# The state's decay diagonal in eight pieces, mean squares by halves, and nine fewer products of constants at the start of a fused RWKV-5 and SwiGLU kernel

## The chip, the cores and the metric

The kernel runs on one core of a Trainium2 chip. The metric is the time of one execution on the device in microseconds (us). Every time of a kernel below is a median over several executions on one chip; times within a kernel are read from one profiled execution. Every run told here was in the fast state. The profile is of one execution, and its span is about 1.8 us shorter than that execution's time (653.1 against 654.93 for one of the changed kernel).

## The reference, cut to what matters

A linear-attention recurrence over 768 steps (4 batches, 8 heads of 48) gives 3072 tokens of 384 features, which go through RMS normalisation and a gated feed-forward layer with 1536 hidden features, all in float32.

```python
for t in range(S):
    kt, vt, rt = (k[:, :, t], v[:, :, t], r[:, :, t])
    cur = np.einsum('bhd,bhe->bhde', u[None] * kt, vt)
    y[:, :, t] = np.einsum('bhd,bhde->bhe', rt, state + cur)
    state = w[None, :, :, None] * state + np.einsum('bhd,bhe->bhde', kt, vt)
# ... y becomes x, (3072, 384)
rms = np.sqrt(np.mean(x * x, axis=-1, keepdims=True) + 1e-06)
xn = x / rms * rms_g
g = xn @ w_gate
silu = g * (1.0 / (1.0 + np.exp(-g)))
return silu * (xn @ w_val) @ w_out
```

## The kernel before

The tokens are cut into 12 blocks of 64 steps (256 tokens with the four batches). The first blocks run while the weights of the feed-forward layer still arrive: they come as 64-bit numbers and are rounded by ScalarE, VectorE and GpSimd together. For this part, which lasts some 155 us, the kernel does not fix the order of the instructions by hand. It describes each piece of work with its engine, an estimated duration, what it reads and what it writes, and a small search at build time looks for a good order:

```python
class Plan:
    HOP = 0.2
    def add(self, engine, cost, reads, writes, give, land=0.0, port=False, name=""):
        ...
    def run(self, cells, first, free, idle=None, trials=3000):
        ...
        rng, best = random.Random(3), None
        for trial in range(trials):
            new = dict(goals)
            ...                                    # a random change of the goals
            start = self.schedule(new, free)
            end = self.replay(start, free)
            end = max(end[i] for i in cells) + 0.3 * sum(end[i] for i in cells) / len(cells)
            if best is None or end <= best[0]:
                best, goals = (end, start), new
        self.start = best[1]
        busy = free["PE"]
        for i in sorted(range(len(self.ops)), key=lambda i: (self.start[i], i)):
            if self.ops[i][0] == "PE":
                if idle and busy < first:
                    idle(self.start[i] - busy)     # products of constants into the gap
                busy = self.start[i] + self.ops[i][1]
            self.ops[i][3]()
```

So every change of a duration or of a dependence can change the order on all engines. The search's `cells` are the two kinds of large products: a gate product (two of them, for the gate and the value, each of 12 passes that use half of the array's rows, 64 of 128) and an output product (12 passes on all 128 rows).

```python
def product(ps_, w, x, start):                     # a gate product: 12 passes of 64 rows
    for cc in range(CC):
        for z in range(2):
            rows = slice(64 * z, 64 * z + 64)
            pe.matmul(ps_[:, z, 0:NT], w[rows, cc, :], x[rows, cc, :], ...)

def add_cell(s, i, hs):                            # an output product: 12 passes of 128 rows
    ...
    for j in range(2):
        for o in range(NQ):
            pe.matmul(po[:, j, 0:DM], hs[o][0][:, j * P : (j + 1) * P], wo[i][:, o, :], ...)

def gate_val(s, i, o):
    # ... two products, then
    add("ACT", 0.38, keys, [f"h{n}"], ..., name=f"silu {s}")
    add("DVE", 0.42, keys, [f"h{n}"], ..., name=f"hm {s}")    # gate times value
```

The parts that the change touches are the diagonal of the state's decay, the mean squares, and the products of constants that keep TensorE warm in the gaps of the first 25 us:

```python
def state_decay():
    for z in range(2):
        rows = slice(64 * z, 64 * z + D)
        for p in range(HP):
            act.mul(KH[rows, z, :, p, :], ...)     # eight instructions of ScalarE

def mean_squares(bank, sq):
    for half in range(2):
        for i in range(CC):
            pe.matmul(bank[:, 2 * P + half : 2 * P + half + 1],
                      sq[:, i, half * P : (half + 1) * P], ones[:, 0:1], ...)

add("ACT", 3.0, ["pw"], ["khd"], state_decay, name="khd")
...
add("PE", 1.35, ["sq0", "sq1"], [key], lambda bank=bank: mean_squares(bank, sq), name=f"r {s}")
...
def warm(us):
    for _ in range(int((us - 0.3) / 0.22)):
        pe.matmul(gv["c"][:, 0, 0:P], ones, ones, start=True, stop=True)
```

Of the kernel before, what the change touches and what calls it, by code (L numbers as in the profile page):

```python
# [49 lines left out]
P = 128  # L50
# [4 lines left out]
def free_dims(t, *dims):  # L55

    return bass.AP(tensor=t.tensor, offset=t.offset, ap=[list(t.ap[0])] + [list(d) for d in dims])
# [3 lines left out]
B, H, S, D = 4, 8, 768, 48  # L61
HP = H // 2
L = 64
NS = S // L
DM, DFF = H * D, 1536
CC = DM // P
# [27 lines left out]
class Plan:  # L94
# [8 lines left out]
    def add(self, engine, cost, reads, writes, give, land=0.0, port=False, name=""):  # L103

        deps = {self.last[r] for r in reads if r in self.last} | {self.last[w] for w in writes if w in self.last}
        for w in writes:
            deps |= self.readers.get(w, set())
        n = len(self.ops)
        if engine in ("DVE", "ACT"):
            cost += 0.03  # L110
        self.ops.append((engine, cost, deps, give, land, port, name))
        for w in writes:
            self.last[w], self.readers[w] = n, set()
        for r in reads:
            if r not in writes:
                self.readers.setdefault(r, set()).add(n)
        return n
# [89 lines left out]
def fast(ctx, tc, chan, tok, vpad, wka, wkb, wot, cols, u_row, out, bad):  # L207
# [8 lines left out]
    pe, dve, act, pool, sp = (InOrder(tc, e) for e in (nc.tensor, nc.vector, nc.scalar, nc.gpsimd, nc.sync))  # L216
# [28 lines left out]
    ones = c_tile([P, P], "ones")  # L245
    dve.memset(ones, 1.0)
    pw = raws.tile([P, HP, L], FP32, name="pw")
# [6 lines left out]
    KH = c_tile([P, 2, B, HP, D], "KH")  # L254
    TOK = c_tile([P, 2, B, HP, D], "TOK")

    ident = c_tile([P, P], "ident")
# [4 lines left out]
    for z in range(2):  # L262
        rows = slice(64 * z, 64 * z + 64)
# [19 lines left out]
    pows = {1: wcol}  # L283
# [20 lines left out]
        act.copy(wk[64:128], ps[64:128, :, 0:D])  # L304
        act.copy(wk[0:64], ps[0:64, :, 64 : 64 + D])

    def state_decay():

        for z in range(2):
            rows = slice(64 * z, 64 * z + D)  # L310
            for p in range(HP):
                act.mul(
                    KH[rows, z, :, p, :], free_dims(ident[rows, 64 * z : 64 * z + D], (0, B), (1, D)),
                    pows[L][rows, p : p + 1],
                )

    def w_range():

# [205 lines left out]
        act.copy(xb[s][64 - 64 * z : 128 - 64 * z], xa[s][64 * z : 64 * z + 64])  # L524


    def mean_squares(bank, sq):
        for half in range(2):
            for i in range(CC):
                pe.matmul(  # L530
                    bank[:, 2 * P + half : 2 * P + half + 1], sq[:, i, half * P : (half + 1) * P], ones[:, 0:1],
                    start=i == 0, stop=i == CC - 1, skip_group_check=True,
                )

    def root(bank, ms):
        act.activation(ms, bank[:, 2 * P : 2 * P + 2], AF.Sqrt, scale=1.0 / DM, bias=eps)
# [65 lines left out]
    p = Plan()  # L602
    add = p.add
# [11 lines left out]
        i = turn["at"] % 2  # L615
        return at[i], f"at{i}"

    add("SP", 0.3, [], ["w"], lambda: None, land=1.9)
    add("DVE", 2.4, ["w"], ["pw"], powers, name="powers")
    add("DVE", 0.43, ["pw"], ["up"], lambda: dve.tensor_mul(up, pw, by_inv), port=True)  # L620
    add("DVE", 0.43, ["pw"], ["down"], lambda: dve.tensor_mul(down, pw_rev, by_inv), port=True)
    add("DVE", 0.22, [], ["dmask"], lambda: dve.tensor_add(dmask, ident[:, 0:64], ident[:, 64:128]), port=True)
# [5 lines left out]
    bank, key = next_at()  # L628
    add("PE", 0.9, ["gdup"], [key], lambda bank=bank: token_powers(bank), name="wk")
    add("ACT", 0.7, [key], ["wk"], lambda bank=bank: keep_token_powers(bank), name="wk")  # L630
    add("ACT", 3.0, ["pw"], ["khd"], state_decay, name="khd")

    def loads(s):
        if s == 0:
# [14 lines left out]
    def mixing(s):  # L649
# [76 lines left out]
                name=f"yT {s}",  # L726
            )
        bank, key = next_at()
        add("PE", 1.35, ["sq0", "sq1"], [key], lambda bank=bank: mean_squares(bank, sq), name=f"r {s}")
        add("ACT", 0.3 if s == 0 else 2.9, [key], ["ms"], lambda bank=bank: root(bank, ms), name=f"sqrt {s}")  # L730
        add("DVE", 0.45, [], ["ms", "diag"], lambda: inverse(ms, diag), name=f"inv {s}")
        add("PE", 0.45, ["diag"], [key], lambda bank=bank: spread(bank, diag), name=f"spread {s}")
# [10 lines left out]
        for z in range(2):  # L743
            add("DVE", 0.95, ["TOKk", "wk"], [f"KH{z}"], lambda z=z: state_k(s, z), port=True, name=f"h {s}")
        last = [next_at() for _ in range(2)]
        add(
            "PE", 1.9, ["KH0", "KH1", "khd", "VSv", "VSs0", "VSs1"], [last[0][1], last[1][1]],
            lambda: [states(last[half][0], half) for half in range(2)], name=f"U {s}",
        )
        for half in range(2):  # L750
# [100 lines left out]

    def warm(us):

        for _ in range(int((us - 0.3) / 0.22)):
            pe.matmul(gv["c"][:, 0, 0:P], ones, ones, start=True, stop=True)

    p.run(cells, 25.0, {"PE": 1.5, "DVE": 1.5, "ACT": 2.5, "POOL": 6.3, "SP": 1.8}, warm)
# [698 lines left out]
```

## Time and profile before

| | before |
|---|---|
| time, median of three | 654.4 us (654.15 to 655.77) |
| span of the profiled execution | 653.1 us |
| TensorE busy | 98% of the span |
| first real product | 9.49 us |
| second load of chan (keys and receptances, by feature) issued, landed | 14.81, 20.46 us |
| first weights product | 27.38 us |
| first output product | 46.4 us |
| main part (the same order in both kernels) begins | 155.8 us |

All but the median are read from the profile. The prediction shows the lines and says how to read them. In the lines, first_a to first_c and at are buffers of sums, hbuf holds gate times value, xa the normalised tokens, wa, wb and wo the weights, and raw, bits and ulp are weights on their way from 64-bit numbers. Three things matter: TensorE has no gap between 52 and 182 us, so the start can only shift what follows; the start is ruled by a chain over DMA, VectorE and ScalarE and not by TensorE; and the DMA engines are nearly full in the first 20 us (a share of 0.90 up to 20.46). One reading was missed then and is shown here, the timeline of TensorE around the first output product. Its columns are start, length, engine, line, work, passes, and in brackets the idle time before it and what ended that:

```profile
44.91 1.50 PE L91 MATMUL at<-ones,sq_first 128*128 128x1 f32 x12 [1.66 <-ACT sq_first L91]
46.27 5.81 PE L91 MATMUL first_b<-wo,hbuf 128*128 128x384 f32 x12
51.92 0.59 PE L91 MATMUL at<-diag,ones 128*128 128x256 f32 x2
```

The output product (second line) takes 5.7 us at half clock instead of about 4. What follows it (third line) needs the diagonal of the inverse root mean squares, which VectorE began at 49.78 and had done at 49.78 + 1.73 = 51.51. With the usual 0.14 us to start, the third line could not have begun before 51.65. So the half clock costs this order only about 0.3 us (an estimate from these lines).

### The profile page before, as it was taken

The numbers are of one execution on the slowest core, as the hardware profiler recorded it, in microseconds if no ns is written. First come the engines' busy times: TensorE is split into PE (matmuls) and PEld (weight loads), VectorE is DVE, ScalarE is ACT, GpSimd is POOL, SyncE is SP. The second block draws the span as 40 slices with busy tenths as digits, with TensorE's granted clock in tenths as the row PEclk, the third lists the DMA queues.
The fourth block names the chain that finished last, engine by engine and source line by source line (L and its number), as shares of the span: only waits on it lengthen the run. The fifth ranks groups of instructions, "written<-read, shape, count | busy, mean of one in ns | idle before, by whom it ended". The sixth has DMA issues, their size and how long they took to land.

```text
span 653.1 us, 15289 instructions
## 1 busy us (share of the span) xinstructions
PE 638.6 (98%) x6534; PEld 504.7 (77%) x6534; DVE 384.7 (59%) x560; ACT 341.9 (52%) x952; POOL 41.7 (6%) x39
## 2 busy tenths in 40 slices
PE   9889999999999999999999999999999999999996
PEld 8868777787878766889766888866888966788753
DVE  6988878855765734765743576653576562555400
ACT  5695465944364653574672564673555582433400
POOL 3154423100000000000000000000000000000000
PEclk9999999999999999999999999999999999999999
DMA  8786643053004242204331404332312321122211
GB/s 260 254 310 213 194 116 115 12 170 78 27 3 167 61 138 49 75 22 166 98 111 40 110 20 158 93 93 73 93 37 101 106 73 25 42 63 73 55 27 28
DMA packets 20398, 64.50 MB, mean 99 GB/s; under 512 B 2912, under 2 KB 6112, under 8 KB 18912
## 3 DMA queue, kind: packets, MB, share of 16 engines
q1 hardware_dynamic: 20320, 63.42, 32.3%
q8 instruction: 53, 0.87, 0.6%
q14 instruction: 25, 0.20, 0.1%
HBM read 58.69 MB, written 4.72 MB: 97 GB/s over the span
## 4 chain that ended last, share of the span: by engine, by line
PE 86%; DVE 5%; ACT 4%; issue 2%; DMA 1%; POOL 0%; DVEq 0%; ACTq 0%; POOLq 0%; SPq 0%
PE po L91 24%; PE b L91 15%; PE a L91 10%; PE c L91 9%; PE first_c L91 5%; PE first_b L91 5%; PE first_a L91 5%; PE at L91 4%; PE py L91 4%; PE pa L91 2%; PE pu L91 2%; ACT ME L91 1%; DVE TOK L91 1%; ACT MO L91 1%; DVE gv L91 1%
## 5 line engine op out<-in xcount | busy, mean ns | idle before, releaser
L91 PE MATMUL po<-wo,h 128*128 128x384 f32 x480 | 159.8, 489 | 0.8 <-DVE bad L91 0.8
L91 PEld LDWEIGHTS po<-wo,h 128*128 128x128 f32 x480 | 90.0, 190 | 60.2 <-PE pc L91 0.8
L91 DVE TENSOR_TENSOR gv<-b,m 128x512 f32<-128x512 f32 x90 | 62.1, 690 | 84.2 <-PE b L91 83.5
L91 ACT ACTIVATE gv<-gv 128x512 f32<-128x512 f32 (+1 forms) x60 | 31.0, 518 | 52.9 <-DVE gv L91 52.9
L91 DVE TENSOR_TENSOR gv<-c,gv 128x512 f32<-128x512 f32 x60 | 41.4, 690 | 15.0 <-PE c L91 14.0
L91 ACT COPY o<-po 128x384 f32<-128x384 f32 x20 | 9.5, 474 | 77.4 <-PE po L91 39.2
L91 ACT ACTIVATE ME<-dmask,du 64x64 f32<-64x64 f32 x176 | 43.8, 330 | 9.8 <-DVE du L91 9.4
L91 PE MATMUL a<-xa,wa 64*128 64x256 f32 x360 | 45.0, 383 | 0.7 <-DVE h L91 0.7
L91 PE MATMUL b<-xa,wa 64*128 64x256 f32 x360 | 44.4, 379 | 0.6 <-DVE gv L91 0.6
L91 ACT ACTIVATE MO<-dmask,du 64x64 f32<-64x64 f32 x176 | 44.4, 334 | 0.7 <-DVE du L91 0.3
L91 PE MATMUL c<-xb,s 64*128 64x256 f32 x360 | 44.3, 378 | 0.0
L91 PE MATMUL b<-t,wb 64*128 64x256 f32 x360 | 44.3, 378 | 0.0
L91 PE MATMUL b<-t,s 64*128 64x256 f32 x360 | 44.0, 377 | 0.3 <-DVE gv L91 0.3
L91 PE MATMUL a<-xb,wb 64*128 64x256 f32 x360 | 43.9, 376 | 0.0
L91 PE MATMUL c<-t,s 64*128 64x256 f32 x360 | 43.9, 376 | 0.0
L91 PEld LDWEIGHTS a<-xa,wa 64*128 64x128 f32 x360 | 33.8, 187 | 7.2 <-DVE h L91 3.0
L91 PEld LDWEIGHTS b<-xa,wa 64*128 64x128 f32 x360 | 34.2, 187 | 6.1 <-DVE gv L91 2.4
L91 PEld LDWEIGHTS b<-t,s 64*128 64x128 f32 x360 | 34.8, 187 | 4.7 <-DVE gv L91 0.7
L91 PEld LDWEIGHTS a<-xb,wb 64*128 64x128 f32 x360 | 34.9, 187 | 4.0
L91 PEld LDWEIGHTS c<-t,s 64*128 64x128 f32 x360 | 34.9, 187 | 4.0
L91 PEld LDWEIGHTS b<-t,wb 64*128 64x128 f32 x360 | 34.5, 187 | 4.1
L91 PEld LDWEIGHTS c<-xb,s 64*128 64x128 f32 x360 | 34.5, 187 | 4.1
(146 smaller groups left out, 1076.0 us busy)
## 6 DMA issues: line engine op xcount, KB each, us to landing
chan<-in_chan_dram SPq DMA_DIRECT2D x11, 1024.0 KB, 5.0
TOK<-in_tok_dram SPq DMA_DIRECT2D x12, 768.0 KB, 4.6
VS<-in_vpad_dram SPq DMA_DIRECT2D x24, 336.0 KB, 4.8
raw<-in_wot_dram SPq DMA_DIRECT2D x8, 576.0 KB, 5.0
out_dram<-o SPq DMA_DIRECT2D x48, 96.0 KB, 2.2
again<-in_wka_dram SPq DMA_DIRECT2D x16, 288.0 KB, 2.8
again<-in_wkb_dram SPq DMA_DIRECT2D x16, 288.0 KB, 2.8
again<-in_wot_dram SPq DMA_DIRECT2D x16, 288.0 KB, 2.8
```

The source lines that it names most:

```text
L91: return lambda *args, **kwargs: self.tc.keep_in_program_order(give(*args, **kwargs))
```

## The change

The intent is to start real work sooner: fewer products of constants ahead of it, a diagonal whose pieces can go between more urgent work on ScalarE, mean squares that start with the first half of the tokens, and two estimates brought nearer to the trace so that the plan sees the early times as they are.

```diff
-    def state_decay():
-        for z in range(2):
-            rows = slice(64 * z, 64 * z + D)
-            for p in range(HP):
-                act.mul(...)
+    def state_decay(z, p):
+        rows = slice(64 * z, 64 * z + D)
+        act.mul(...)                               # one of the eight
...
-    def mean_squares(bank, sq):
-        for half in range(2):
-            for i in range(CC):
+    def mean_squares(bank, sq, half):
+        for i in range(CC):
...
-    add("SP", 0.3, [], ["w"], lambda: None, land=1.9)
-    add("DVE", 2.4, ["w"], ["pw"], powers, name="powers")
+    add("SP", 0.3, [], ["w"], lambda: None, land=1.1)
+    add("DVE", 1.75, ["w"], ["pw"], powers, name="powers")
...
-    add("ACT", 3.0, ["pw"], ["khd"], state_decay, name="khd")
+    for z in range(2):
+        for i in range(HP):
+            add("ACT", 0.34, ["pw"], [f"khd{z}{i}"], lambda z=z, i=i: state_decay(z, i), name="khd")
...
-        add("PE", 1.35, ["sq0", "sq1"], [key], lambda bank=bank: mean_squares(bank, sq), name=f"r {s}")
+        for half in range(2):
+            add("PE", 0.7, [f"sq{half}"], [key],
+                lambda bank=bank, half=half: mean_squares(bank, sq, half), name=f"r {s}")
...
     def warm(us):
-        for _ in range(int((us - 0.3) / 0.22)):
+        for _ in range(int((us - 0.3) / 0.22) - (9 if us > 4 else 0)):
```

(The reader of `khd` in the diff waits for all eight keys; that line is left out.)

More of the change, by code (lines that the diff above doesn't have):

```diff
@@ L305, in keep_token_powers @@
         act.copy(wk[0:64], ps[0:64, :, 64 : 64 + D])
-    def state_decay():
-        for z in range(2):
-            rows = slice(64 * z, 64 * z + D)
-            for p in range(HP):
-                act.mul(
-                    KH[rows, z, :, p, :], free_dims(ident[rows, 64 * z : 64 * z + D], (0, B), (1, D)),
-                    pows[L][rows, p : p + 1],
-                )
+    def state_decay(z, p):
+        rows = slice(64 * z, 64 * z + D)
+        act.mul(
+            KH[rows, z, :, p, :], free_dims(ident[rows, 64 * z : 64 * z + D], (0, B), (1, D)), pows[L][rows, p : p + 1]
+        )
     def w_range():
@@ L524, in exchange @@
         act.copy(xb[s][64 - 64 * z : 128 - 64 * z], xa[s][64 * z : 64 * z + 64])
-    def mean_squares(bank, sq):
-        for half in range(2):
-            for i in range(CC):
-                pe.matmul(
-                    bank[:, 2 * P + half : 2 * P + half + 1], sq[:, i, half * P : (half + 1) * P], ones[:, 0:1],
-                    start=i == 0, stop=i == CC - 1, skip_group_check=True,
-                )
+    def mean_squares(bank, sq, half):
+        for i in range(CC):
+            pe.matmul(
+                bank[:, 2 * P + half : 2 * P + half + 1], sq[:, i, half * P : (half + 1) * P], ones[:, 0:1],
+                start=i == 0, stop=i == CC - 1, skip_group_check=True,
+            )
     def root(bank, ms):
@@ L728, in mixing @@
         bank, key = next_at()
-        add("PE", 1.35, ["sq0", "sq1"], [key], lambda bank=bank: mean_squares(bank, sq), name=f"r {s}")
+        for half in range(2):
+            add(
+                "PE", 0.7, [f"sq{half}"], [key], lambda bank=bank, half=half: mean_squares(bank, sq, half),
+                name=f"r {s}",
+            )
         add("ACT", 0.3 if s == 0 else 2.9, [key], ["ms"], lambda bank=bank: root(bank, ms), name=f"sqrt {s}")
@@ L746, in mixing @@
         add(
-            "PE", 1.9, ["KH0", "KH1", "khd", "VSv", "VSs0", "VSs1"], [last[0][1], last[1][1]],
+            "PE", 1.9, ["KH0", "KH1", "VSv", "VSs0", "VSs1"] + [f"khd{z}{i}" for z in range(2) for i in range(HP)], [last[0][1], last[1][1]],
             lambda: [states(last[half][0], half) for half in range(2)], name=f"U {s}",
```

## The prediction

> **What bounds the kernel now.** I read the whole span first, then cut it into stages, then followed the chain of waits through the first stage. The page gives TensorE as busy for nearly all of it:
>
> ```profile
> span 653.1 us, 15289 instructions
> PE 638.6 (98%) x6534; PEld 504.7 (77%) x6534; DVE 384.7 (59%) x560; ACT 341.9 (52%) x952; POOL 41.7 (6%) x39
> ```
>
> That 98% contains work which is no work: products of a constant with itself, issued into gaps of the start. So I asked for the busy times by stretch; the columns are the stretch, its length, busy time of TensorE, weight loads, VectorE, ScalarE and GpSimd, granted clock, DMA share and GB/s:
>
> ```profile
> 20.00:27.40 7.40, 6.64 (x108) 6.25 (x106) 6.63 (x11) 4.30 (x9) 1.01 (x1) 1.00 0.73 240
> 27.40:46.30 18.90, 15.22 (x248) 12.98 (x245) 15.88 (x23) 17.89 (x59) 8.79 (x7) 1.00 0.90 306
> 46.30:52.10 5.80, 5.80 (x14) 3.25 (x15) 5.48 (x8) 3.48 (x5) 2.91 (x2) 0.71 0.63 189
> 52.10:182.00 129.90, 129.90 (x1372) 104.36 (x1373) 94.78 (x129) 70.01 (x183) 23.84 (x16) 1.00 0.37 110
> 182.00:653.00 471.00, 462.23 (x4506) 359.87 (x4502) 247.77 (x355) 235.44 (x674) 0.00 (x0) 1.00 0.26 76
> ```
>
> From 52.1 to 182 us TensorE never stops, and afterwards it is busy 462 of 471 us. That part does the same products in both kernels (after the first blocks the orders of all engines agree), so it can only begin earlier or later. The change plays in the first 50 us. There, the timeline of TensorE (start, length, work, passes; two passes are one product) begins:
>
> ```profile
> 1.16 8.40 PE L91 MATMUL first_c<-ones 128*128 128x128 f32 x50 [1.16 <-DVE pw L91]
> 9.49 1.15 PE L91 MATMUL first_a<-chan,hbuf 48*64 48x64 f32 x32
> 10.57 0.66 PE L91 MATMUL at<-ident,gdup 128*128 128x128 f32 x4
> 11.15 1.15 PE L91 MATMUL first_a<-chan,hbuf 48*64 48x64 f32 x32
> 12.23 0.49 PE L91 MATMUL first_c<-ones 128*128 128x128 f32 x2
> ```
>
> Real work starts at 9.49, only because the 25 constant products end then: its inputs were there earlier (ScalarE finished the keys times u at 6.64, and VectorE's wait for the r half of chan ended at 6.63). What follows is in the chain that ended last:
>
> ```profile
> 12.72 2.04 PE at L91 x64
> ...
> 14.81 5.65 DMA chan<-in_chan_dram
> ...
> 20.58 1.24 DVE ME L91
> ...
> 23.26 0.18 DVE ms L91
> ```
>
> The scores of the first block end at 14.76 and release the buffer of chan; its second load lands at 20.46; VectorE, strictly in order, decays r and k of block 1 from it before it inverts the root mean squares of block 0 at 23.26; xa of block 0 follows at 24.80, and the first real weights product at 27.38.
>
> **What the Trainium skill says.** "TensorE: Matmul & The Clock Gate", Part 1, says that the array starts at half clock and is released after some 3.4 us of activity, in a free-running window. The trace agrees in kind: the constant products' passes take 428 ns in the mean up to 6 us and 275 ns from 7.5 us on, and their starts go from about 0.21 us apart (22 begun by 6.0) to 0.11 us (50 by 9.45). The release comes at about 6.2 us, 5 us after the first one; the profile's granted clock reads 1.00 all along, so it doesn't show this. The same part says that idle brings the half clock back, which is why fillers exist. In the trace it does: after 1.66 us idle and 1.5 us of one-column products (43.3 to 46.4 us) the clock reads 0.50 from 47.8 to 50.5. "DMA: Bandwidth & Descriptors", section on the anatomy of one DMA, says that waits for semaphores lie on the issuing sequencer, not on the DMA engines. The trace agrees: the chan load is issued at 14.81, 0.05 us after the scores end, and everything behind it on that queue was held too (the next load is issued at 15.18).
>
> **The change, part by part.** I compared both orders, since the scheduler decides anew. Constant products fall from 25+1+9+2+6+5 = 48 to 15+6+5+6+5 = 37.
>
> *Fillers at the start.* 30 passes instead of 50. The trace has 29 passes begun by 7.0 and 32 by 7.3, so 30 are over at about 7.15: the first real product moves by 9.49 - 7.15 = 2.3 us. That is ten products at 0.23, no more than the full-clock rate. The half-clock ones stay.
>
> *The lone filler before the scores* goes: 0.4 us (12.23 to 12.65). Sum for the scores: 2.7 us, so they would end at 12.05.
>
> *Decay diagonal in eight pieces.* Eight ScalarE instructions either way, 2.97 us together. In the kernel before they run from 6.55 to 9.42, and the first copy of decayed r waits behind them, harmless while TensorE waits for 9.49. In the new order four pieces go ahead of that copy, one before the second copy, three after it. The first copy moves to about 6.55 + 4 x 0.37 = 8.05, the second to about 10.0 to 10.6. Scores halves would start at 9.95 and 11.0, so neither copy binds. Undivided, the second copy would end at about 11.25 (9.42 + 0.6 + 0.64 + 0.6), later than 11.0: the split saves about 0.3 us of this.
>
> *Mean squares by halves.* The three products of each half wait for their own squares already. In blocks 0 to 2 the new order has the halves adjacent: worth 0. Only block 3 separates them, where TensorE is full anyway.
>
> *The load of chan* is issued 2.75 us earlier. But the DMA engines are full: 0.9 to 1.05 of share from 3 us on, and of the bytes asked for by 14.81 only 3.7 MB were in (the GB/s of stretches of one microsecond, added up). It now goes ahead of the fourth weight piece (0.39 MB), whose load had left before it. In the old trace 4.21 MB precede it, it has 1.05 MB, and it landed when 5.77 MB had come, so 65% of the 0.79 MB issued just after it got in between. Now 3.81 + 1.05 + 0.65 x 1.18 = 5.63 MB. At the trace's rate of about 0.41 MB per us, without the dip at 16 to 17 us (163 GB/s, the bubble before this load's first bytes), that is reached at about 19.2. So 1.3 us is kept of 2.7: R of block 1 starts at 19.3 instead of 20.58. VectorE's own work ahead of it (20.31 in the old trace, less 2.4) would be done at 17.9.
>
> *VectorE behind it.* One piece of weight conversion (0.35 us) goes from before the reciprocal to after it: reciprocal at 21.7 instead of 23.26, xa at 23.2 instead of 24.80. The root's ScalarE instruction now precedes the 1.04 us copy of block 1, but VectorE comes later than either. First stretch: 1.6 us earlier.
>
> *The second stretch, 27 to 46 us,* is ScalarE's: 17.89 busy of 18.90, 32 diagonal products of 8.0 us, then the weights' low words. It inherits 1.4 to 1.6 us. Its new order puts the table load and one Silu before three of these conversions, and moves one yT group behind the squares. I get the squares of block 1 done at about 43.6 instead of 45.2, and TensorE's stream beginning 1.6 us earlier. Sum: 1.6 us. If the half clock at 47.8 to 50.5 goes as well, 1.4 us more (half of 2.7); I count a third of that, 0.4. The filling of the pipeline behind 50 us depends on conversions on VectorE and GpSimd, which I allow to eat nothing on balance. 654.4 - 1.6 - 0.4 = 652.4.
>
> **Rivals.** First, that the transfer hides everything: chan lands when the DMA engines have moved what is ahead, and if all three later pieces go in first (6.04 MB), it lands at 20.5 and nothing but the 0.35 us is won: 654. For it speaks a DMA share of 1; against it, that the load leaves 2.7 us earlier and ahead of a piece. Second, that the gain comes whole: the load gets in with 4.86 to 5.3 MB, R starts at 18 to 18.5, and the half clock vanishes: 650.5 to 651. Third, that less filling cools the array: my times leave TensorE idle from about 20.0 to 22.3, against 0.76 us in the old trace. The products behind it at half clock would cost 1 to 1.5 us, and the new order could stall on weights after 50 us, where the old one doesn't stall at all: 654 to 655.5. Against that, U and the first weights product there wait for VectorE and ScalarE anyway.
>
> **Range and chances.** The centre is 652.4. The rivals span 650.5 to 655.5, and three runs of the old kernel differ by 1.6 us; eight in ten in 650.5 to 654.8. Two per cent is 13 us, which neither all constant products together (48 at 0.23 to 0.43, 11 to 20 us, most of them beside waits) nor a whole stall could give. Within 2%: 0.98.
>
> **What would show it.** First real product at 7.1 to 7.2; scores over by 12.1; chan landing at 18.5 to 20.0; reciprocal at about 21.7; TensorE without gaps from about 43 to 45 us. A chan landing at 20.5 proves the first rival, a granted clock of 0.50 in 20 to 30 us the third. The prediction is wrong if TensorE has new waits of more than 1 us between 50 and 155 us, since all gains sit ahead of that.

## The result and the profile after

The changed kernel takes 655.25 us (654.87 to 655.61, four runs), the one before 654.37 us in the same rounds. The ratio is 1.0009, with a 95% interval of 0.9992 to 1.0026: the same. Ratios here are the mean time of one kernel's fast runs over that of the other's of the same rounds, so not quite the ratio of the medians that are quoted. The range of 650.5 to 654.8 did not hold it.

The first page of the profile shows the same span as before, with 22 passes fewer (6534 - 6512), which are 11 products of constants (nine by the edit, two by the new order):

```profile
span 653.1 us, 15238 instructions
PE 636.7 (97%) x6512; PEld 500.8 (77%) x6512; DVE 383.7 (59%) x560; ACT 342.5 (52%) x952; POOL 43.3 (7%) x39
```

The start did move. The timeline of TensorE has the constant products, and the first real one behind them:

```profile
1.16 5.10 PE L91 MATMUL first_c<-ones 128*128 128x128 f32 x30 [1.16 <-DVE pw L91]
6.80 1.15 PE L91 MATMUL first_a<-chan,hbuf 48*64 48x64 f32 x32 [0.54 <-ACT hbuf L91]
```

The constants end 0.54 us before their successor has its input, so the first product is bound by ScalarE in this execution, and starts 2.7 us earlier than at 9.49. There is some luck in that: the same 15 constant products took 5.10 us here, because the clock was released at about 4.3 us, and 6.57 us in e4 below, where it was released at about 7.4 and the first product came at 7.65. The chain of waits of the changed kernel goes on with the load, the first use of it on VectorE, and the reciprocal of the roots:

```profile
11.63 7.22 DMA chan<-in_chan_dram
...
18.98 1.23 DVE ME L91
...
21.34 0.09 DVE ms L91
```

The load is issued 3.2 us earlier (14.81 to 11.63) and lands 1.6 us earlier (20.46 to 18.86). The reciprocal and the first weights product (at 25.37 instead of 27.38) are 2.0 us earlier; in the other profiles with this start (e4, e5, e6, e10, e13) it came at 25.30 to 26.13. Up to here the change does what it was made for. The busy times by stretch (columns as in the prediction) show the rest of the start:

```profile
20.00:27.40 7.40, 6.38 (x111) 5.50 (x111) 7.22 (x13) 4.61 (x11) 1.01 (x1) 1.00 0.61 201
27.40:46.30 18.90, 14.45 (x229) 11.91 (x226) 16.09 (x24) 18.68 (x57) 9.96 (x8) 0.97 0.91 310
46.30:52.10 5.80, 5.80 (x20) 3.33 (x20) 5.70 (x8) 2.47 (x5) 3.09 (x3) 0.80 0.86 258
```

TensorE is busy 0.77 us less than before in the second stretch (14.45 instead of 15.22), although its work there starts earlier, and the granted clock still falls below 1 (0.97 and 0.80). The timeline of TensorE shows where the time went:

```profile
42.32 1.50 PE L91 MATMUL at<-ones,sq_first 128*128 128x1 f32 x12 [0.36 <-ACT sq_first L91]
45.67 5.60 PE L91 MATMUL first_b<-wo,hbuf 128*128 128x384 f32 x12 [1.85 <-DVE hbuf L91]
```

The mean squares of block 1 start 2.6 us earlier than before (42.32 against 44.91). But the output product behind them, which followed at once before, now waits 1.85 us for VectorE. The timeline of VectorE says what it did in that time:

```profile
40.69 1.87 DVE L91 SCALAR_TENSOR_TENSOR bits<-raw,bits 128x576 int32<-128x576 int32 x1
42.48 0.45 DVE L91 TENSOR_SCALAR bits<-raw 128x576 int32<-128x576 int32 x1
42.96 1.86 DVE L91 SCALAR_TENSOR_TENSOR bits<-raw,bits 128x576 int32<-128x576 int32 x1
...
45.11 0.41 DVE L91 TENSOR_TENSOR hbuf<-first_b,hbuf 128x256 f32<-128x256 f32 x1
45.44 0.41 DVE L91 TENSOR_TENSOR hbuf<-first_c,hbuf 128x256 f32<-128x256 f32 x1
```

It converted weights. In the kernel before, the first two of the three products of this kind were done before the squares ended, and the third came in time for the output product that had begun:

```profile
43.41 0.41 DVE L91 TENSOR_TENSOR hbuf<-first_a,hbuf 128x256 f32<-128x256 f32 x1
43.75 0.41 DVE L91 TENSOR_TENSOR hbuf<-first_b,hbuf 128x256 f32<-128x256 f32 x1
46.32 0.42 DVE L91 TENSOR_TENSOR hbuf<-first_c,hbuf 128x256 f32<-128x256 f32 x1 [0.96 <-ACT hbuf L91]
```

In the changed kernel the two short products that the output product needs stand behind four conversions, and two of these took 1.87 and 1.86 us where the same instruction takes 0.75 at 38.72. GpSimd was adding weights in that time (40.30 to 41.94 and 42.70 to 44.21), and both ended some 0.6 us after its addition did. A conversion with one input went from 0.45 to 1.27 us in the same way (39.39, beside an addition that began at 38.87). The Trainium skill, "GPSIMD Engine Reference", section 1 (specifications), says that GpSimd shares its interfaces to the buffer memory with VectorE, with contention for VectorE instructions that have two inputs there; this one has two, and the trace agrees.

The second loss is further on. Cut at the end of the first output product and at the beginning of the main part, TensorE's busy time by stretch (columns as in the prediction) reads, before:

```profile
51.92:155.82 103.90, 103.90 (x1133) 81.12 (x1131) 77.23 (x104) 58.81 (x151) 23.84 (x16) 1.00 0.40 122
```

and after:

```profile
51.20:155.94 104.74, 104.74 (x1131) 80.86 (x1130) 73.34 (x101) 60.04 (x155) 24.03 (x15) 1.00 0.40 122
```

Neither has a gap nor a lower clock, and the work is the same, yet the new order needs 0.84 us more (some 0.9, since the first stretch reaches 0.06 us into the main part, which begins at 155.76). What differs is the order: TensorE changes 23 times between gate products and others in the first stretch and 29 times in the second, counted in the traces with the change into the main part. (The recorded expectations give 8 more for every kernel, 31 and 37 here; counted over this stretch the traces don't have them. The differences between kernels are the same.) The balance of the two profiled executions, every term from the starts above: up to the first weights product 2.0 us gained, from there to the mean squares 0.6 more; from the mean squares to the output product 2.0 lost (1.36 us between the two starts before, 3.35 after); the output product the same; behind it 0.8 lost. The sum is a loss of 0.1 to 0.2, and the main part begins at 155.9 instead of 155.8. The rest of the 0.9 us between the medians is not in these two executions, whose spans are equal.

Part of the spread between executions goes with the clock. A stretch at half clock takes 3.41 us and so costs up to 1.7, and takes 0.26% off the mean clock (1.7 of 653). In one kernel of the study (run e11 below), executions with spans of 652.0, 652.9 and 654.6 us had mean clocks of 0.997, 0.994 and 0.991. But five executions of e10 with the same mean clock, 0.995, had spans of 652.1 to 654.9, so it is not all of it. In all 16 profiles the clock also falls at the very end of the kernel: between 648 and 652 us the granted clock was 0.96 in the profile before, 0.68 in the one after and 0.50 in that of e11. So differences below 1 us between medians are read here with the trace beside them.

### The profile page after: what moved, and what is told of

Same layout as the page of the kernel before. It is cut to its first block, busy times and chain, and to the rows that moved or that the text cites. A ratio compares the mean times of both kernels' runs of the same rounds, so it can differ in the third digit from the quotient of the medians.

```text
span 653.1 us, 15238 instructions
## 1 busy us (share of the span) xinstructions
PE 636.7 (97%) x6512; PEld 500.8 (77%) x6512; DVE 383.7 (59%) x560; ACT 342.5 (52%) x952; POOL 43.3 (7%) x39
## 4 chain that ended last, share of the span: by engine, by line
PE 85%; ACT 6%; DVE 5%; issue 2%; DMA 1%; ACTq 0%; DVEq 0%; SPq 0%
PE po L91 24%; PE b L91 15%; PE a L91 10%; PE c L91 9%; PE first_b L91 5%; PE first_a L91 5%; PE first_c L91 4%; PE py L91 4%; PE at L91 3%; PE pa L91 2%; ACT ME L91 2%; PE pu L91 2%; ACT MO L91 2%; DMA chan<-in_chan_dram 1%; DVE gv L91 1%
```

## The experiments

The theory after the first reading had three parts: the earlier start is real and passes through the load of chan; TensorE loses it behind the mean squares of block 1 because the plan puts two urgent products of VectorE behind conversions; and the new order costs more where half-array and full-array products change more often. The rivals were that the cut itself harms (a cooler array), that one of the two splits does it, or that nothing but the spread is seen. Each part is done alone or undone. An overview, all beside runs of the kernel before on the same chip (whose medians were 654.04, 654.24, 654.38 and 654.61 us in the four batches):

| run | what it is | time, median | ratio to before, 95% interval |
|---|---|---|---|
| changed | at the prediction | 655.25 | 1.0009, 0.9992 to 1.0026 |
| e10 | changed, again | 655.43 | 1.0011, 0.9993 to 1.0029 |
| e1 | before with the cut alone | 654.65 | 1.0008, 0.9993 to 1.0024 |
| e11 | e1 again | 654.77 | 1.0004, 0.9989 to 1.0019 |
| e2 | changed without the cut | 655.87 | 1.0021, 1.0008 to 1.0035 |
| e7 | changed with no first constants | 655.94 | 1.0025, 1.0011 to 1.0038 |
| e9 | before with mean squares by halves | 656.26 | 1.0032, 1.0013 to 1.0051 |
| e13 | changed, eight pieces together | 655.23 | 1.0001, 0.9982 to 1.0020 |
| e4 | changed, two gate products sooner | 653.34 | 0.9987, 0.9973 to 1.0001 |
| e5 | changed, two tiny products together | 668.64 | 1.0217, 1.0203 to 1.0231 |
| e6 | changed, two tiny products apart | 672.24 | 1.0263, 1.0249 to 1.0277 |
| e3 | changed, changes priced in the plan | 654.47 | 1.0001, 0.9987 to 1.0014 |
| e8 | e3 and gate products sooner | 653.02 | 0.9971, 0.9957 to 0.9984 |
| e12 | before with the cut and one load later | 653.14 | 0.9978, 0.9963 to 0.9994 |
| e14 | e12 with constants before the squares | 653.01 | 0.9969, 0.9955 to 0.9983 |

By the study's bar of 2%, every one but e5 and e6 counts as the same as the kernel before; the intervals say more. The times forecast by the theory held for e5, e7, e10, e12 and e13, and e4 was faster than forecast. They did not hold for e1, e2, e3, e8 and e9, nor for the 6 us between e5 and e6 (3.6 by the medians); e14 fell on the side of its rival. For e11 the median held, but not the late landing of the load.

**The cut alone (e1, repeated as e11), and everything but the cut (e2).**

```diff
 # e1, e11: the kernel before with this line alone; e2: the changed kernel with it taken back
-        for _ in range(int((us - 0.3) / 0.22)):
+        for _ in range(int((us - 0.3) / 0.22) - (9 if us > 4 else 0)):
```

> The kernel before with one edit: 9 of the 25 constant products at the start left out; all orders stay as before (31 changes between gate products and other products on TensorE after the first output product). Theory A (the cut's early gain is real, the changed kernel lost it again in its new orders): first real product at about 6.8 us, scores over at about 12.3 (the undivided diagonal holds the second copy), chan still behind the fourth weight piece and landing at about 19.4 to 19.8 instead of 20.46, reciprocal about 1 us earlier than 23.26, first output product at about 45.4 instead of 46.41, and as no change of kind is added, about 1 us kept to the end: 653.4 us. Rival B (what is won at the start is hidden by the transfer or by later waits in any order): 654.2 to 654.6. Rival C (everything passes through): 652.0 or less.

> The changed kernel with the 9 constant products put back (24 at the start), orders untouched. Theory A: first real product at about 9.0 us instead of 6.80, chan landing 1.0 to 1.5 us later than 18.86, everything to the first output product later by as much, 656.2 to 656.7 us. Rival B (hidden): 655.2, no change.

> The kernel before with only the nine constant products cut, once more, because its five times lay 3.0 us apart and its profile fell on the slowest. Theory A2 (formed on that profile: without the new load order the transfer hides the cut, and the longer wait of TensorE then lets the clock fall in some executions): chan lands at 20.4 or later, first output product at 46 us or later, times again 1.5 us or more apart, median 654.0 to 655.0. Rival (that profile was an accident): chan at about 19.5, and a median of 653.4 or less.

The profiled execution of e1 was its slowest: the load of chan took 9.06 us instead of 5.65, and two stretches ran at half clock (25 to 29 and 49 to 53 us). That is why it was repeated. In the trace of e11 the load landed at 19.5 and the first weights product began at 26.43, 1.0 us earlier than before, and the main part began at 154.61, some 1.1 us earlier. In the medians little or nothing of this is seen (ratios 1.0008 and 1.0004), and the executions of e11 have mean clocks from 0.997 down to 0.991, where those of the kernel before lay mostly at 0.995 to 0.997. So the cut shifts the start; that part of this goes to more time at half clock fits these clocks, but is not shown. With e2 the new orders start at the old time: its first weights product is at 26.68, its first output product at 46.96 (46.27 before) and its main part at 157.44. The new orders alone are a loss of 0.2%, and the cut wins about half of it back.

**No first constants at all (e7).**

```diff
-        for _ in range(int((us - 0.3) / 0.22) - (9 if us > 4 else 0)):
+        for _ in range(0 if us > 4 else int((us - 0.3) / 0.22)):
```

> The changed kernel without any constant product in the first gap. Theory A (these products only serve to bring the clock up): the first real product at 6.8 us as with 15 of them, but at half clock until about 11.8, scores over at 12.5 to 14 instead of 11.57, chan 0.5 to 1.5 us later, 655.7 to 656.7 us. Rival (the small products of the start are bound by something other than the clock, or the transfer hides it): 655.2, no change.

The chain of waits of e7 has the first real products:

```profile
6.39 1.97 PE first_a L91 x32
```

They start 0.4 us earlier than in the changed kernel and take 1.97 us instead of 1.15, because the array still runs at half rate. The scores end at 13.96 instead of 11.57, the products of block 0 behind them run until 19.89 and hold up the decay of block 1 (18.98 in the changed kernel), and the first weights product is at 26.26 instead of 25.37. The constants that the change left are needed in this order; without them the ratio is 1.0025.

**The mean squares by halves alone (e9).**

```diff
 # the kernel before with
-        add("PE", 1.35, ["sq0", "sq1"], [key], lambda bank=bank: mean_squares(bank, sq), name=f"r {s}")
+        for half in range(2):
+            add("PE", 0.7, [f"sq{half}"], [key], ..., name=f"r {s}")
```

> The kernel before with only the mean squares split by halves, which alone already makes the scheduler settle on other orders (35 changes between kinds instead of 31, fillers 44). Theory A: the split is worth nothing by itself, the orders decide: four more changes at 0.2 us make a stream about 0.8 us longer; 654 to 656 us. Rival (the halves let the mean squares finish earlier): 653 us or less.

This split alone gives the slowest of the kernels without added work, 1.0032. No instruction of the start is lengthened by it. The search takes another order: 27 changes between gate products and others instead of 23, and 104.69 us of busy time between the first output product and the main part instead of 103.90. The profiled execution had no half clock around the output product, and the main part still began at 156.44 (0.99 us of it idle behind the output product). (The two new estimates alone were built too, and left the order as it was; they were not run. The eight pieces alone in the kernel before were not tried either; whether they too move the order is not shown.)

**The eight pieces together again (e13).**

```diff
 # in the changed kernel, once the search is over
         self.start = best[1]
+        pieces = [i for i, op in enumerate(self.ops) if op[6] == "khd"]
+        for n, i in enumerate(pieces):
+            self.start[i] = self.start[pieces[0]] + 1e-6 * n
```

> The changed kernel with one thing altered: on ScalarE the eight pieces of the diagonal stand together ahead of the first copy of the gates' first product (as the undivided diagonal did), and everything else is left. If the pieces let the copies in between them start sooner and that carries through: copies end some 0.5 to 1 us later, the channel-mix load is issued later by as much, and the time is over 656.2 us. If the pieces have no effect by themselves, because the load's landing is set by the bytes ahead of it (5.6 MB by 18.9 us): scores end at most 0.3 us later than the 11.6 us of the changed kernel, the load lands within 0.3 us of 18.9, and the time is 655.0 to 655.9 us, within the spread of the changed kernel.

The chain of waits:

```profile
12.54 6.25 DMA chan<-in_chan_dram
...
18.91 1.22 DVE ME L91
```

The first copy on ScalarE now starts at 9.37 instead of 8.11, the scores end 0.9 us later (12.47 against 11.57; I had expected at most 0.3), and the load is issued 0.9 us later. It lands at 18.79, against 18.86 in the changed kernel: 6.25 us in flight instead of 7.22. So the last 0.9 us of the earlier start buys nothing, which fits the bytes ahead of the load setting its landing. The repetitions agree: in e4, e5, e6 and e10, which have the same order of loads, it was issued between 11.45 and 12.41, and VectorE's first use of it began between 19.03 and 19.48; the earliest issue led to 19.33, later than the 18.91 here. Everything behind it agrees within 0.15 us (main part 156.08 against 155.94), and the time is that of the changed kernel, 655.23 us. Within this order the pieces have no effect of their own. This is the first rival of the prediction in a weaker form: the transfer hides not all of the earlier start but what goes beyond some 2 us of it.

**Two products of VectorE sooner (e4).**

```diff
         self.start = best[1]
+        for i in [i for i, op in enumerate(self.ops) if op[6] == "hm 0"][1:3]:
+            self.start[i] = max(self.start[d] for d in self.ops[i][2]) + 1e-6
```

> The changed kernel with two VectorE products (second and third gate of the first cell) moved ahead of weight conversions, TensorE's order the same. Theory A (the 1.0 us between 36 and 46 us was lost because these two stood behind the conversions on VectorE): the first output product starts at about 44.0 us instead of 45.67, the end 1.2 to 1.6 us earlier, about 653.8. Rival (the later weights bind then, or the half clock costs it): the first output product starts earlier, but the stream gets a wait of about as much before 56 us, and the time is 655.0 to 655.5.

The timeline of TensorE:

```profile
43.41 1.50 PE L91 MATMUL at<-ones,sq_first 128*128 128x1 f32 x12
44.77 4.12 PE L91 MATMUL first_b<-wo,hbuf 128*128 128x384 f32 x12
```

The wait is gone: the output product follows the mean squares at once. It also runs at full clock here; the half clock fell into 38 to 41.5 us. By the ratios it is 0.22% or 1.4 us below the changed kernel (0.9987 against 1.0009), and the main part begins 1.4 us sooner (154.55). This confirms the wait as a loss. It is not the whole of the 1.85 us, since TensorE then idles 0.45 us for the diagonal of block 1 and 0.23 us for xa, and is busy 105.06 us behind the output product. The mixed gain holds two terms, which the trace lets apart: 1.99 us for the wait (1.36 us from the squares to the output product instead of 3.35) and 1.49 for the clock (4.04 us from the output product to the next instead of 5.53), less the 0.68 idle and 0.31 more busy behind them. Of these 2.5 us 1.1 are lost again, because the squares start at 43.41 instead of 42.32 in this execution, with its later first product and its half clock before them.

**The price of a change between half-array and full-array products (e5, e6).** Before each gate product, two tiny products on all 128 rows are added: both ahead of the first half (e5), or one ahead of each half (e6). The instructions are the same in number and kind, the changes differ. e6's result is wrong (relative error 0.28), which I had not foreseen and which does not touch its time: the start flag of the second tiny product falls into an open sum of the same bank. The Trainium skill, "PSUM — Partial Sum Buffer", section "The four PSUM rules", says that the start flag of a second open group clears the marks of the first, whose next product then overwrites its partial sum; the error agrees with that.

```diff
+    def tiny(ps_):
+        pe.matmul(ps_[:, 1, 500:501], ones, ones[:, 0:1], start=True, stop=True, skip_group_check=True)
...
-            lambda: product(ps_, wa[i][:, o], xa[s], True), name=f"g {s} {i} {o}",
+            lambda: [tiny(ps_), tiny(ps_), product(ps_, wa[i][:, o], xa[s], True)], name=f"g {s} {i} {o}",
 # e6: tiny(ps_) once there, and once ahead of product(ps_, wb[i][:, o], xb[s], False)
```

> The changed kernel with two tiny full-array products (one column, into an unused column) ahead of each of the 24 gate blocks of the start: 63 changes between gate products and other products after the first output product instead of 37. By itself it only sets the base for the next run: 48 tiny products at about 0.2 us and 26 changes at about 0.2 us, less the first six, which lie beside waits: 666 to 670 us.

> The same 48 tiny products, one ahead of each half of a gate block instead of two ahead of the block: the same instructions, 93 changes instead of 63. Theory A (each change between half-array gate products and full-array products costs TensorE about 0.2 us in a stream without gaps): 30 x 0.2 = 6 us longer than with the tiny products together, 4.5 to 8. Rival (the longer first block after a change is only how the trace models ends, or overlaps): less than 1 us.

The chain of waits has blocks of 28 passes (two halves of 12 and the tiny ones, two passes each), in e5:

```profile
90.28 3.33 PE first_c L91 x28
```

and in e6:

```profile
91.81 3.62 PE first_c L91 x28
```

So one more turn to a full-array product and back costs 3.62 - 3.33 = 0.29 us here, less than the 0.4 that two lengthened neighbours suggested. Over the whole stretch, e5 has 55 changes between gate products and others and e6 has 85. TensorE was busy 117.65 us in e5 and 121.79 us in e6 from the end of the first output product to the main part: 4.14 us for 30 changes, 0.14 each. The medians differ by 3.6 us. The changes cost this without any more work. The six more that the changed kernel has than the one before come to 6 x 0.14 = 0.8 us (an estimate), the size of the loss that was found.

**The price put into the plan (e3), and with the gate products sooner (e8).** The search knew no such price. In e3, the changed kernel's plan adds 0.2 us to a gate product behind any other and to most others behind a gate product, and starts from another seed. Price and seed were not tried apart.

```diff
+    def turns(self, kind, i):
+        now = self.ops[i][6][:1]
+        if now == "g":
+            return 0.2 if kind not in ("g", None) else 0.0
+        return 0.2 if kind == "g" and now in "Prs" else 0.0
...
+            if e == "PE":
+                end[i] += turns(kind, i)
+                kind = self.ops[i][6][:1]
...
-        rng, best = random.Random(3), None
+        rng, best = random.Random(6), None
 # e8: this, and the lines of e4 with [0:3] instead of [1:3]
```

> The changed kernel, whose scheduler now counts 0.2 us for each such change (and draws from another seed): 27 changes instead of 37, the other orders of the start change too. Theory A: the stream from the first output product to the first product of the main part is 10 x 0.2 = 2 us shorter than the 110.3 us of the changed kernel, so about 108.3, unless it gets idle gaps; time 652.8 to 653.8 us. Rival (the changes cost nothing): a stream of 110 us and 654.5 to 655.5 us.

> As the run before, and with the first cell's three gate products on VectorE put right behind what they wait for. If both losses are as theory A has them, they add: the first output product at about 44 us, the stream at about 108.3 us, 651.5 to 652.5 us, ahead of both kernels. Rival (weights bind once the stream starts sooner): no better than the better of the two alone, 653 us or more.

The new order has 19 changes, fewer than either kernel. The stretch behind the output product in e3 reads:

```profile
51.23:154.97 103.74, 103.12 (x1131) 81.44 (x1130) 75.56 (x101) 57.22 (x150) 22.75 (x15) 1.00 0.37 114
```

It is 103.12 us of busy TensorE, 1.6 less than the changed kernel, and 0.6 us idle. Together with e9 and the two kernels this gives a series for the same products in four orders, without any half clock:

| changes between gate products and others | 19 (e3, e8) | 23 (before, e11, e12) | 27 (e9) | 29 (changed, e10, e13, e2) |
|---|---|---|---|---|
| TensorE busy from the first output product's end to the main part, us | 103.12 to 103.13 | 103.90 to 103.92 | 104.69 | 104.74 to 104.75 |

Four more changes cost 0.8 us twice, 0.2 each, and the last two hardly anything; from 23 to 29 that is 0.14 each, as in e6 against e5. The orders differ in more than the count, and e4, with the changed kernel's order and two short waits in it, needs 105.06, so differences of a few tenths say little in this table. e3 is the same as before by its median all the same (1.0001), and e8 is faster than before (0.9971, interval 0.9957 to 0.9984), although their two profiles are nearly alike: the main part begins at 154.97 and 155.01. In e8 the output product begins at 45.52, no earlier than in e3 (45.48), so moving the gate products won nothing there. What parts their medians is not in the profiled executions, and not in the clock either: the mean over the five executions is 0.9948 in e3 and 0.9952 in e8, which is worth some 0.3 of the 1.45 us. It stays open.

**The old order with the cut and one later load (e12), and with constants before the squares (e14).** The changed order also puts the load of chan ahead of the fourth piece of the weights. In e12 the kernel before gets that and the cut, nothing else.

```diff
 # e12: the kernel before with the cut of e1, and
         self.start = best[1]
+        at = {op[6]: i for i, op in enumerate(self.ops)}
+        self.start[at["load 3"]] = self.start[at["load chan 1"]] + 1e-6
 # e14: e12, and ahead of the mean squares of block 1
+            for _ in range(6 if s == 1 else 0):
+                pe.matmul(gv["a"][:, 0, 0:P], ones, ones, start=True, stop=True)
```

> The run before with one more edit: the load of the fourth weight piece is issued behind the load of chan, as in the changed kernel; all five engines' orders else as in the kernel before. Theory A2 (the load order, not the cut, let the start's gain through, and the new orders behind it lost it again): chan lands at about 19 us, reciprocal at 21.5 to 22, first output product at 44.5 to 45.2, stream as in the kernel before (109.4 us, or 1.4 less if the half clock stays away), 652.3 to 653.3 us, better than the changed kernel by about 2 us. Rival (a start that is 1.5 us earlier is lost in any order): 654 us or more.

> The run e12 (old orders, cut of the nine products, fourth piece of the weights loaded behind the channel-mix load) with six more products of constants on TensorE right before block 1's mean squares, where it idles about 1.6 us. If that idle is what brings the stretch at half clock (46 to 50 us, first output product 5.4 us long instead of 4.1): the stretch is gone, the output product takes 4.1 us, and the time is about 651.9 us, 1.3 below that of e12. If the stretch comes from something else (the clock is reviewed on its own rhythm, or idle elsewhere counts): the output product still takes 5.4 us and the time is that of e12, about 653.1 us.

> The changed kernel once more, unaltered, so that the runs beside it compare on one chip. Theory A: profile as before: chan landing near 18.9 us, first output product near 45.7, stream of 110.3 us; 654.9 to 655.6 us, ratio 1.000 to 1.002.

In e12 the load lands at 19.15, the first weights product is at 26.06 and the main part at 154.22, 1.5 us before that of the kernel before. The ratio of 0.9978 agrees with that, and its interval ends below 1. It does not start as early as the changed kernel, but keeps all it has, because its order behind 42 us is the old one. Between e11 and e12 only the place of one load differs. In the traces that is 0.4 us (main part at 154.61 and 154.22), in the medians 1.6; the lower mean clocks of e11 (0.9943 against 0.9957 over six executions) account for about 0.9 of this as an estimate, and why they differ was not looked into. The changed kernel, repeated beside it as e10, gave 1.0011.

The timeline of TensorE in e12 shows why an absent half clock is worth little in the old order:

```profile
44.92 4.12 PE L91 MATMUL first_b<-wo,hbuf 128*128 128x384 f32 x12
50.30 0.67 PE L91 MATMUL at<-diag,ones 128*128 128x256 f32 x2 [1.26 <-DVE diag L91]
```

The product takes 4.12 us instead of 5.81, and then TensorE waits 1.26 us for VectorE's diagonal. What was written beforehand for e14 had a wrong premise: it took the 5.4 us between these two starts for a product at half clock. There was none in that profiled execution, nor in that of e11, and both had 1.64 us idle right before the squares, as the kernel before had (1.66, with half clock). In e14, six constants fill this idle time, the product takes 4.12 us too, and the wait behind it is 0.93 us; from the first weights product to the main part e12 takes 128.16 us and e14 128.18. The medians, 653.14 and 653.01, are the same. The mean clock over the six executions of e14 is 0.998, of e12's 0.996, which is what filling the gap would do, but the times don't show it beyond their spread. So whether that idle time brings the half clock stays open: it isn't enough for it. Where the clock's window falls may play a part. In each of the 16 profiles the changes of the granted clock lie whole multiples of 3.413 us apart, and the last such window ahead of the half clock was 44.09 to 47.50 in the kernel before (TensorE busy for 2.59 us of it); the windows around the same products were 43.38 to 46.79 in e11 (2.86) and 43.17 to 46.58 in e12 (3.02), with no half clock after. The busy time alone is not the rule: in e9 a window with 1.79 (42.29 to 45.71) had no half clock after it.

Three versions beat the kernel before in their rounds: e14 (0.9969), e8 (0.9971) and e12 (0.9978), all of them correct; only e12 had the changed kernel beside it (e10, 1.0011).

## Why the prediction was wrong

**What held.** The early chain did, step by step: first real product at 6.80 (7.15 predicted; bound by ScalarE and not by the constants as predicted, thanks to the early release of the clock), scores over at 11.57 (12.05), landing at 18.86 (19.2) with 5.64 MB in (5.63), reciprocal at 21.26 to 21.34 (21.7), xa at 22.78 (23.2), and 2.0 us gained at the first weights product where 1.4 to 1.6 were counted (1.3 to 2.1 over the profiles with this start). That the pieces don't set the landing was right (e13), though for the scores they are worth 0.9 us, not the 0.3 counted. The first rival, that the transfer hides the gain, was rightly put down as partial. The third rival's cooler array did not come about between 20 and 30 us in the changed kernel (clock 1.00), though it did in one execution of the cut alone.

**The step that failed first** is "TensorE's stream beginning 1.6 us earlier". It carried the gain of the chain to the squares of block 1 (right, and even 2.6 us in the trace) and from there to the output product, taking for granted that this follows the squares as before. I followed ScalarE in that stretch because it was busy 17.89 of 18.90 us, and did not look at the order of VectorE, where the new plan had put the two gate products behind conversions that slow down beside GpSimd. The output product began 0.7 us earlier instead of 1.6 (46.41 to 45.67 in the chain). e4 shows that moving the two products takes the wait away.

**The second** is "The filling of the pipeline behind 50 us depends on conversions on VectorE and GpSimd, which I allow to eat nothing on balance." I looked there for stalls, and there were none in the changed kernel, so the prediction's own sign of being wrong, waits of more than 1 us between 50 and 155 us, did not show. The loss is inside the stream without a gap: 0.84 us more of busy time for the same products, and the order changes more often between half-array and full-array products, which e6 against e5 shows to cost that much. The Trainium skill, "TensorE: Matmul & The Clock Gate", Part 3, "The mechanism", says that loading weights overlaps products in flight only where these use other rows of the array; a full-array product leaves no other rows, which fits, but no run here looks into it. The chain of waits of the kernel before has both kinds beside each other:

```profile
72.32 3.87 PE first_a L91 x12
...
80.56 1.50 PE first_a L91 x12
82.06 1.29 PE first_b L91 x12
...
91.12 4.07 PE first_b L91 x12
```

An output product behind gate products takes 4.07 us, one behind another output product 3.87; the first gate block behind other work 1.50, the next ones 1.29. In the changed kernel's chain the mean squares and spreads stand scattered in between, and 1.50 appears again and again:

```profile
102.66 1.23 PE at L91 x12
103.89 3.98 PE first_c L91 x12
107.87 1.50 PE first_b L91 x12
109.36 0.63 PE at L91 x2
109.99 1.50 PE first_b L91 x12
```

All of this could have been read beforehand: the lengths stand in the old trace, and the order of the changed kernel was there to count.

**The third** is the term of 0.4 us for the half clock. It did not vanish (0.50 from about 45.3 to 48.7 us, and the output product took 5.6 us as before). The 1.4 us counted for its absence was read from the old order, where it is only about 0.3, since VectorE's diagonal ends the wait anyway (e11 and e12: 1.26 to 1.28 us idle in its place). In the changed order a gate product follows at once, and e4 gains 1.49 there and loses 0.99 behind it, so the 0.4 that was put in would have been about right, as an estimate.

The sum: 0.9 us from the first step (1.6 less 0.7), 0.8 from the second, 0.4 from the third are 2.1 of the 2.85 us between 652.4 and 655.25. The rest lies between single executions, and the traces don't show where. That the time would stay within 2% was right, for the reason given there.

## What to carry to other kernels

When a search makes the order, a small change of the start is judged by the new order of every engine, up to the point from which the orders agree: compare what each late product waits for, on the engine that isn't the bound too. A stretch in which TensorE never stops is not of fixed length; count how often its products change between half and whole array, and give the plan that price (here, with another seed, that took 1.6 us off the stretch, though e3's median didn't show it). And before a wait or a slow stretch is booked as a gain, look at what would end next behind it: the diagonal of VectorE took the place of the half clock in the old order, and the bytes ahead took that of the scores.

## What the Trainium skill lacked or had wrong

- "TensorE: Matmul & The Clock Gate", Part 3, has no figure, and "TensorEngine Tiling (Array Packing)", section "Key Properties", has none either, for a change between float32 products on half the rows and on all rows. Here a gate block of 12 passes took 1.50 us behind other work and 1.29 us behind its like, an output product 4.07 against 3.87, and a turn there and back, measured by itself, 0.29 us (30 changes: 4.14 us).
- "TensorE: Matmul & The Clock Gate", "HAM oscillation", speaks of idle gaps longer than about 3.4 us. Here the half clock came behind gaps of 1.66 us or less in a sparse stretch of products (kernel before), and stayed away behind nearly the same gap (1.64 us, e11 and e12). The length of a stretch, 3.41 us in the traces, agrees with its Part 1.
- The same page, Part 1, puts the release of the clock at the start around 4 us into the activity, give or take 0.5. Here it came 3.1 us after the first product in the changed kernel, 5.4 in the kernel before and 6.2 in e4. The profile's granted clock doesn't show the half rate there (it reads 1.00 while the first products of e7 take 1.97 us instead of 1.15).
